# Opening tile's fourth head pair turned earlier, first products on PSUM tiles of their own, second tile's keys turned on two PSUM tiles and its queries last

## The chip, the cores and the metric

The kernel runs on one core of a Trainium2 chip. The metric is device time in microseconds (us), lower is better; before the change three runs gave 329.65, 330.06 and 330.78 us, median 330.06. A core has a matrix engine (PE, with its weight loads shown as PEld), a vector engine (DVE), an activation engine (ACT), a general engine (POOL) and a queue engine (SP). Each runs its own instructions strictly in the order in which they are written; engines wait for one another on semaphores. POOL also issues most of the input transfers, so whatever waits on POOL holds up the transfers queued behind it.

## The reference

Sliding-window causal attention (8 batches, 8 heads, 576 positions, head size 64, window 64), followed by a gated feed-forward block on 4608 tokens of 512 channels:

```python
scores = scale * np.matmul(q, k.transpose(0, 1, 3, 2))
mask = (rel >= 0) & (rel < window)
scores = np.where(mask, scores, -1000000000.0)
attn = np.exp(scores - max); attn = attn / (sum + 1e-09)
x = matmul(attn, v)   # heads side by side: 4608 x 512
g = x @ w_gate
out = ((g * sigmoid(g)) * (x @ w_val)) @ w_out   # d_ff = 1536
```

(Shortened; `max` and `sum` run over the keys.)

## The kernel before

**Tiles.** The 4608 tokens are nine tiles of 512: tile t is the first 512 positions of batch t, and tile 7 (LAST) gathers the last 64 positions of all batches. For each tile the kernel makes scores, exponentials and totals, multiplies by V (the mix), divides by the totals (`scale`, DVE, L385, which writes xT), runs twelve gate/value steps (`gate_value`, eight matmuls of 128x128 by 128x512 each; L429) and then the output projection (`project`, L438), which for tile t is woven into the attention of tile t+1. `gate_end` turns a step's two PSUM results into a slice of hT: a SiLU on ACT (L422), then a product on DVE (L423). The eight heads are handled as four pairs, u = 0 to 3.

**PSUM.** There are eight banks. Banks 0 and 1 belong to one tile, `two[0]`, banks 2 and 3 to `two[1]`; banks 4 to 7 are tiles of their own (`one0` to `one3` in the instruction order, all shown as `one` in the profile). Waits are made per tile: a write to bank 1 waits for a reader of bank 0. `out_tile()` and `d_tile()` alternate between banks 4/5 and 6/7 by counters in `taken`; a gate/value step takes one of each.

**Opening.** Tile 0 is read in fp32 and cast (`cast_first`, L544). Its q and k are turned by PE transposes (`turn_first`, L195), whose results are copied to queries and keys by DVE (L553 and, as `split_k`, L198). A bias for the mask is put into PSUM by matmuls (`bias_first`, L227), the scores are added (`scores_first`, L240), ACT takes the exponential (`weigh_first`, L558), totals come from matmuls with ones (`sums_first`, L295), and ACT inverts them by a logarithm (L316) and an exponential (L319). The products with V (`part_first`, L348) come in three passes, even, odd and late, with a tiny matmul and a tiny DVE copy (`marker`, `seen`) between the first two, which serve as a fence. Pair 3 is turned last (L195 at 12.5 us), its products go to bank 5 and are woven into the first gate matmuls (`gate_part`, L409), which run as soon as each pair is scaled.

**Second tile.** Tile 1's keys come in bf16 as `raw_k` (shown as k_r) and are turned on PE between gate steps 6 and 7 (pairs 0 and 1, banks 0 and 1) and between steps 8 and 9 (pairs 2 and 3, banks 2 and 3), L677, each followed by a DVE copy (L198). Its queries are turned by DVE itself (`turn_q`, L207), after half of each block has been moved between partitions (`second_halves`, L118: once on ACT, twice on POOL, once on DVE). From tile 2 on, DVE turns both (`turn`: L207 and L217), four pairs per tile, after chosen gate steps (`turns`).

**Transfers.** POOL's queue issues, in order, V of tile 0, the gate and value weights in blocks of 256 columns, tile 1's keys and queries among them, the output weights, V of tile 1, then q and k of tile 2. An issue waits for the landing of the transfer eight places earlier.

Of the kernel before, what the change touches and what calls it, by code (L numbers as in the profile page):

```python
# [10 lines left out]
BF16 = mybir.dt.bfloat16  # L11
# [6 lines left out]
def kernel(  # L18
# [10 lines left out]
    nc = tc.nc  # L29
# [24 lines left out]
    v1 = v12[:, 0]  # L54
# [21 lines left out]
    def load_runs(eng, dst, src, t, hs):  # L76
        eng.dma_start(
            dst.rearrange("r h e d -> r h (e d)"),
            src[batch(t), hs, 0:512].rearrange("h (r e) d -> r h (e d)", e=4),
        )  # L80
# [24 lines left out]
    def load_plain(t, us):  # L105

        for a in range(2):
            nc.gpsimd.dma_start(
                staged[t][0][64 * a:64 * a + 32, us],
                q[batch(t), a + 2 * us.start:2 * us.stop:2, 0:512]  # L110
                .rearrange("u (r e) d -> r u (e d)", e=16),
            )

    def second_halves(t, us, a, copy):

        src, dst = slice(64 * a, 64 * a + 32), slice(64 * a + 32, 64 * a + 64)
        ap = staged[t][0][:, us].rearrange("r u (e d) -> r (u e) d", d=D)
        copy(ap[dst, :, 0:32], ap[src, :, 32:64])  # L118
# [60 lines left out]
    def weights_gv(f0, f1, c0=0, c1=4):  # L179
        for src, dst in ((moe_w_gate, wg), (moe_w_val, wv)):  # L180
            nc.gpsimd.dma_start(
                dst[:, c0:c1, f0:f1],
                src[P * c0:P * c1, f0:f1].rearrange("(c r) f -> r c f", r=P),
            )

    def weights_o(c0, c1):
        nc.gpsimd.dma_start(
            wo[:, c0:c1, :],
            moe_w_out[P * c0:P * c1].rearrange("(c r) f -> r c f", r=P),
        )  # L190
# [3 lines left out]
        for e in range(4):  # L194
            nc.tensor.transpose(tp[:, P * e:P * e + P], src[:, e], identb[:])  # L195

    def split_k(dst, tp):
        nc.vector.tensor_copy(  # L198
            dst.rearrange("p (r e) -> p r e", e=4),
            tp.rearrange("p (e r) -> p r e", e=4),  # L200
        )
# [20 lines left out]
    def bias_first(u):  # L222

        for c in range(2):
            for h in range(2):
                r = slice(64 * h, 64 * h + 64)
                nc.tensor.matmul(  # L227
                    two[u % 2][64 * c:64 * c + 64, h], identb[r, r],
                    bias[r, c ^ h].rearrange("r e i c x -> r (e i c x)"),
                    start=True, stop=False,  # L230
                )
# [109 lines left out]
    def part_first(us, banks, x, ms):  # L341

        for u, b in zip(us, banks):
            E = weights[0, u]
            for m in ms:
                r = slice(0, P) if m % 2 else half(x)
                for h in range(2):
                    nc.tensor.matmul(  # L348
                        blocks(bank[b][half(h)], 0, m, m + 1),
                        v1[r, m // 2 if m % 2 or not x else m // 2 - 1, 2 * u + h, :],  # L350
                        blocks(E[r, h, :], 0, m, m + 1),
                        start=m + x == 0, stop=(m, x) == (6, 1),
                    )
# [153 lines left out]
    def keep_warm(n):  # L507
        for _ in range(n):
            nc.tensor.matmul(warm[0:D], ones[:, 0:D], ones[:])
# [33 lines left out]
    def cast_first(copy, u, i):  # L543
        copy(  # L544
            first[:, i, u].rearrange("r e (h d) -> r h e d", h=2),
            raw[i][:, 2 * u:2 * u + 2],
        )

    def turn_first(u, banks):
        tps = [bank[b].bitcast(BF16)[:, 0:512] for b in banks]  # L550
        for i in range(2):
            transposes(tps[i], first[:, i, u])
        (on_v if u else on_a)(queries[0][:, u, :], tps[0])  # L553
        split_k(kT[0][:, u, :], tps[1])
# [6 lines left out]
    def sums_first(u, b):  # L561
        totals_first(u, bank[b])
        inverse[0, u] = room(1)[:, 0]
        return lambda: log(inverse[0, u], bank[b]), lambda: invert(inverse[0, u])
# [12 lines left out]
    cast_first(on_a, 2, 0)  # L577
    cast_first(on_p, 3, 0)
    weights_gv(0, 256, 0, 2)
    on_p(v1[:, 0], v_first[:, 0])  # L580
    on_p(v1[:, 1], v_first[:, 1])
    weights_gv(0, 256, 2, 4)
    weights_gv(256, 512)
    weights_gv(512, 768)
# [5 lines left out]
    load_runs(nc.gpsimd, raw_k[:, 0:4], k, 1, slice(0, 4))  # L590
    weights_gv(1024, 1280)
    load_runs(nc.gpsimd, raw_k[:, 4:8], k, 1, slice(4, 8))
    load_plain(1, lo)
    weights_gv(1280, 1536)
    weights_o(0, 2)
    second_halves(1, lo, 1, on_p)
    load_plain(1, hi)
    weights_o(2, 4)
    weights_o(4, 8)
    weights_o(8, 12)  # L600
    load_halves(nc.gpsimd, vb[1], 1, range(3))
# [1 line left out]
    load_halves(nc.gpsimd, vb[1], 1, range(3, H))  # L603

    cast_first(on_v, 2, 1)
    bias_first(1)
    log0, inv0 = sums_first(0, 6)
    scores_first(1)
# [2 lines left out]
    inv0()  # L611
    keep_warm(1)
    turn_first(2, (4, 5))
    cast_first(on_v, 3, 1)
    bias_first(2)
    keep_warm(1)
    log1, inv1 = sums_first(1, 7)
    scores_first(2)
    log1()
    weigh_first(2)  # L620
    turn_first(3, (4, 5))
    bias_first(3)
    scores_first(3)
    weigh_first(3)
    inv1()
    even, odd, late = (0, 2, 4, 6), (1, 3, 5, 7), (2, 4, 6)
    log2, inv2 = sums_first(2, 6)
    part_first(range(3), (0, 1, 4), 0, even)
    marker(7)
    nc.vector.tensor_copy(seen[:], bank[7][0:D, 0:1])  # L630
    part_first(range(3), (0, 1, 4), 0, odd)
    marker(7)
    part_first(range(3), (0, 1, 4), 1, late)
    log2()
    inv2()
    part_first((3,), (5,), 0, even)
    log3, inv3 = sums_first(3, 7)
    log3()
    inv3()
    part_first((3,), (5,), 0, odd)  # L640
    pairs = [(bank[2], bank[3]), (bank[6], bank[0])]
    scale(0, 0, bank[0])
    scale(0, 1, bank[1])
    gate_part(0, (0, 1), pairs, 0)
    marker(7)
    part_first((3,), (5,), 1, late)
    gate_part(0, (0, 1), pairs, 1)
    for u in (2, 3):
        scale(0, u, bank[u + 2])
    for c in range(2, 4):  # L650
        gate_part(0, (0, 1), pairs, c)
    taken["v"] = 1
    set_silu()
    for m in range(12):
        if m < 2:
            gate_end(0, m, pairs[m])
        else:
            gate_value(0, m)
        if m == 2:
            for x in range(2):  # L660
                for c in range(2):
                    nc.vector.tensor_copy(
                        mask[half(x), 0, c],
                        tri[half(x), x ^ c].rearrange("r (y e) -> r e y", e=16),
                    )
            for i in (1, 2, 4):
                nc.vector.tensor_copy(mask[:, i:2 * i], mask[:, 0:i])
            for E in eb:
                nc.vector.memset(E[:, 0], 0.0)
        if m == 8:  # L670
            second_halves(1, lo, 0, on_a)
        if m in (6, 8):
            for u in (m - 6, m - 5):
                tp = bank[u].bitcast(BF16)[:, 0:512]
                for e in range(4):
                    for h in range(2):
                        nc.tensor.transpose(  # L677
                            tp[half(h), P * e:P * e + P], raw_k[:, 2 * u + h, e], identb[:]
                        )
                split_k(kT[1][:, u, :], tp)  # L680
        if m in (9, 10):
            turn_q(1, m - 9)

    set_exp()
    second_halves(1, hi, 0, on_v)
# [4 lines left out]
    def columns(c0, c1):  # L690
        project_part(0, range(4), tiles, range(c0, c1))

    scores(1, 0)
    columns(0, 4)
    scores(1, 1)
    columns(4, 7)
    for w in range(2):
# [9 lines left out]
    for t in range(1, NT):  # L707
        if t > 1:
            set_exp()
            scores(t, 0)  # L710
            project(t - 1, 0)
            if t == 2:
                stage_v(3)
            o_ps = out_tile()
            project_part(t - 1, (1,), (o_ps,), range(5))
            scores(t, 1)
            sums(t, 0)
            project_part(t - 1, (1,), (o_ps,), range(5, 12))
            project_end(t - 1, 1, o_ps)
            project(t - 1, 2)  # L720
            sums(t, 1)
            mix_all(t)
            project(t - 1, 3)
        set_silu()
        if t + 1 == LAST:
            load_last_v()
        elif t + 1 < NT and t > 1:
            cast_v(t + 1)
        if t + 2 < NT:
            load_qk(t + 2)  # L730
            if t > 1 and t + 2 != LAST:
                stage_v(t + 2)
        if t == 2:
            k_l = load_k(
                cast.tile([P, 4, 4, 4 * D], BF16, name="k_l", tag="c0"),
                [(b, S - P) for b in range(4, 8)],
            )
        turns = (6, 8, 10, 11) if t == 1 else (1, 4, 7, 10)
        for m in range(12):
            gate_value(t, m)  # L740
            if m in turns and t + 1 < NT:
                turn(t + 1, turns.index(m))
            if m == 8 and 3 <= t < 7:
                turn_k(kT[2], k_l, t - 3)
# [32 lines left out]
```

## Time and profile before

| What | us |
|---|---|
| Median of three runs | 330.06 |
| The profiled execution, its own time | 330.95 |
| Its span, first to last instruction | 329.2 |
| PE busy | 318.4 (97%) |
| DVE busy | 217.8 (66%) |
| ACT busy | 165.8 (50%) |
| POOL busy | 148.4 (45%) |
| Granted PE clock, mean | 1.000 |

The profiled execution is 0.89 us longer than the median of the runs, and 1.75 us of it lie outside the span. Rows of the timeline read: start, duration, engine, line, operation, out<-in, shape, count, and in brackets the idle time before it and what ended it. Consecutive matmuls overlap: one 128x512 matmul takes 0.38 us, but the next starts 0.216 us after it, so 16 of them fill 3.46 us, and a gate/value step of eight fills 1.73 us. The chain of work that ended last is read from the end backwards to what released each piece.

### The profile page before, as it was taken

To read this page: it belongs to the slowest core of one execution; us is meant where nothing else is said; L and a number is where in the kernel's file an instruction comes from. 1 tells how busy PE (TensorE), PEld (TensorE's weight loads), DVE (VectorE), ACT (ScalarE), POOL (GpSimd) and SP (SyncE) were. 2 spreads that over 40 slices of the span, in tenths; PEclk is the share of its full clock that TensorE was granted. 3 is DMA by queue.
4 is the path that set the end of the run, shared out by engine and by line. 5 is a ranking of instruction groups with operands and counts; after the bars stand their busy time and mean duration, and the time that the engine had idled before them with its cause. 6 is when DMAs were issued, how large, how long until landed. Compare 5 with 4: busy or idle time off the path is not lost.

```text
span 329.2 us, 7015 instructions
## 1 busy us (share of the span) xinstructions
PE 318.4 (97%) x2739; PEld 151.8 (46%) x2782; DVE 217.8 (66%) x344; ACT 165.8 (50%) x237; POOL 148.4 (45%) x263
## 2 busy tenths in 40 slices
PE   7998899999999999999999999999999999999995
PEld 4544444444444454445444444445444544444443
DVE  3565575479767776687669767876787666774422
ACT  4762367435833574356535663475337633683310
POOL 4872956887055697556422989474110000000000
PEclk9999999999999999999999999999999999999999
DMA  7999999999589999969950999899601300021013
GB/s 244 178 176 198 165 164 183 197 150 131 116 157 197 163 152 181 205 69 183 219 86 7 140 195 99 57 175 191 127 3 26 91 16 0 9 81 44 0 24 105
DMA packets 83522, 40.36 MB, mean 123 GB/s; under 512 B 64160, under 2 KB 78752, under 8 KB 83488
## 3 DMA queue, kind: packets, MB, share of 16 engines
q0 software_dynamic: 51488, 22.59, 57.8%
q1 hardware_dynamic: 31456, 16.79, 21.0%
q10 hardware_dynamic: 544, 0.52, 0.5%
q8 instruction: 21, 0.34, 0.4%
q14 instruction: 13, 0.11, 0.1%
HBM read 53.02 MB, written 9.44 MB: 190 GB/s over the span
## 4 chain that ended last, share of the span: by engine, by line
PE 93%; DVE 4%; issue 1%; DMA 1%; ACT 0%; DVEq 0%
PE one L429 55%; PE one L438 27%; PE two L269 2%; PE two L369 2%; PE one L302 1%; DMA q_f<-in_q_dram 1%; DVE hT L423 1%; PE one L195 1%; PE two L409 1%; PE one L480 1%; DVE kT L198 1%; PE two L240 0%; DVE kT L217 0%; DVE qT L207 0%; PE two L227 0%
## 5 line engine op out<-in xcount | busy, mean ns | idle before, releaser
L422 ACT ACTIVATE sg<-one 128x512 f32<-128x512 f32 x107 | 63.9, 597 | 116.8 <-PE one L429 90.8
L423 DVE TENSOR_TENSOR hT<-sg,one 128x512 bf16<-128x512 f32 x106 | 73.6, 694 | 62.3 <-PE one L429 61.4
L429 PE MATMUL one<-xT,wg 128*128 128x512 bf16 x415 | 108.4, 379 | 0.9
L429 PE MATMUL one<-xT,wv 128*128 128x512 bf16 x415 | 107.2, 379 | 0.1
L438 PE MATMUL one<-wo,hT 128*128 128x512 bf16 x396 | 93.5, 380 | 1.5 <-issue 0.3
L126 POOL DMA_DIRECT2D k_s<-in_k_dram x112 | 60.7, 549 | 24.2 <-DMA q_s<-in_q_dram 16.6
L429 PEld LDWEIGHTS <-wv 128*128 128x128 bf16 x424 | 41.5, 98 | 50.0
L429 PEld LDWEIGHTS <-wg 128*128 128x128 bf16 x424 | 41.3, 98 | 49.9 <-issue 0.3
L438 PEld LDWEIGHTS <-hT 128*128 128x128 bf16 x420 | 39.1, 98 | 46.5 <-issue 1.8
L282 ACT ACTIVATE eb<-two 128x960 bf16<-128x960 f32 (+1 forms) x32 | 29.5, 974 | 15.9 <-PE two L269 15.8
L217 DVE STREAM_TRANSPOSE kT<-k_s 128x512 bf16<-128x512 bf16 x28 | 36.1, 1288 | 0.0
L285 DVE TENSOR_TENSOR eb<-eb,mask 128x960 bf16<-128x960 bf16 (+1 forms) x32 | 21.1, 659 | 11.7 <-ACT eb L282 11.6
L177 POOL CAST vb<-v_f 128x512 bf16<-128x512 f32 x20 | 11.5, 619 | 36.9 <-DMA v_f<-in_v_dram 14.7
L385 DVE TENSOR_TENSOR xT<-two,r 128x512 bf16<-128x512 f32 x34 | 21.7, 686 | 6.4 <-PE two L369 4.8
L319 ACT ACTIVATE r<-r 128x512 f32<-128x512 f32 (+1 forms) x34 | 22.3, 655 | 1.0
L207 DVE STREAM_TRANSPOSE qT<-q_s 128x512 bf16<-128x512 bf16 x32 | 22.4, 703 | 0.1
L316 ACT ACTIVATE r<-one 128x512 f32<-128x512 f32 x32 | 18.9, 590 | 6.1 <-PE one L302 5.3
L91 POOL DMA_DIRECT2D q_s<-in_q_dram x24 | 13.0, 556 | 4.7 <-DVE qT L207 4.7
L290 DVE TENSOR_TENSOR both<-eb 128x512 bf16<-128x512 bf16 x32 | 13.6, 425 | 1.1
L152 POOL DMA_DIRECT2D vb<-in_v_dram x16 | 11.1, 715 | 4.6 <-DMA vb<-in_v_dram 2.0
L488 ACT ACT_TABLE_LOAD x9 | 11.5, 1283 | 2.0 <-issue 1.9
L98 POOL DMA_DIRECT2D q_s<-in_q_dram x16 | 8.6, 627 | 7.0 <-DVE qT L207 7.0
(117 smaller groups left out, 197.4 us busy)
## 6 DMA issues: line engine op xcount, KB each, us to landing
k_s<-in_k_dram POOLq DMA_DIRECT2D x112, 56.0 KB, 4.8
q_s<-in_q_dram POOLq DMA_DIRECT2D x24, 248.0 KB, 5.3
v_f<-in_v_dram SPq DMA_DIRECT2D x40, 128.0 KB
wg<-in_moe_w_gate_dram POOLq DMA_DIRECT2D x5, 256.0 KB, 8.1
wv<-in_moe_w_val_dram POOLq DMA_DIRECT2D x5, 256.0 KB, 8.7
q_f<-in_q_dram SPq DMA_DIRECT2D x4, 256.0 KB
wo<-in_moe_w_out_dram POOLq DMA_DIRECT2D x2, 512.0 KB, 9.0
vb<-in_v_dram POOLq DMA_DIRECT2D x16, 64.0 KB, 5.4
```

Source lines behind the costliest of these rows:

```text
L126: nc.gpsimd.dma_start(k_s[p0:p0 + 32, g, :, 0:w], k[b, a:H:2, s:s + P].rearrange("u (r e) d -> r u (e d)", e=4) [:, :, 32 * c:32 * c + w],)
L207: nc.vector.transpose(queries[t][:, u, :].rearrange("r (e x) -> r e x", e=16), staged[t][0][:, u].rearrange("r (e d) -> r e d", d=D)[:, :, ...
L217: nc.vector.transpose(dst[:, u, :].rearrange("r (g x e) -> r g e x", g=4, e=4), k_s[:, :, u].rearrange("r g (e d) -> r g e d", d=D)[:, :, ...
L282: nc.scalar.activation(flat, s_ps[h][:].rearrange("r a b -> r (a b)")[:, 0:n], AF.Exp, scale=0.125)
L285: nc.vector.tensor_mul(flat, flat, mask[:].rearrange("r j c e y -> r (j c e y)")[:, 0:n])
L316: nc.scalar.activation(r, d_ps, AF.Ln)
L319: nc.scalar.activation(r, r, AF.Exp, scale=-1.0)
L385: nc.vector.tensor_mul(x, o_ps, r)
L422: nc.scalar.activation(sg[:], g_ps[:], AF.Silu)
L423: nc.vector.tensor_mul(hT[t][:, m, :], sg[:], v_ps[:])
L429: nc.tensor.matmul(ps[:], w[:, c, P * m:P * m + P], xT[t][:, c, :], start=(c == 0), stop=(c == 3),)
L438: nc.tensor.matmul(o_ps[:], hT[t][:, c, P * s:P * s + P], wo[:, c, :], start=(c == 0), stop=(c == 11),)
```

## The change

- Pair 3's key cast moves up on DVE, and its transposes move ahead of pair 1's totals and pair 2's scores, on banks 6 and 7. Pair 1's totals go to bank 2 (in `two[1]`). Two filler matmuls (`keep_warm`) become one.
- The two casts of tile 0's V leave POOL for DVE, after the last key copy.
- The products of pairs 0 to 3 go to banks 4, 5, 0 and 1, with pair 3's even products ahead of the fence. The first gate matmuls are no longer woven with products: after all products come 16 in a row, on banks 2 and 3 (`two[1]`) and 4 and 6.
- Tile 1's keys: pairs 0 and 1 are still turned after step 6, pairs 2 and 3 now after step 9; the two pairs of a step stand in `two[0]` and `two[1]`. The copies after step 9 are on ACT instead of DVE.
- Tile 1's queries: loads and half moves are issued later on POOL's queue (behind the last gate weights and the first output weights); the half move of pairs 0 and 1 that was POOL's is DVE's, after step 9; ACT's half move and both turns stand after step 10 instead of at steps 8, 9 and 10.
- The first column of the projection of tile 0 (four matmuls) stands ahead of tile 1's first scores.
- Tile 2's turns during tile 1 stand after steps 6, 7, 9 and 10 instead of 6, 8, 10 and 11.

```diff
--- before.py
+++ after.py
@@ -194,8 +194,8 @@
         for e in range(4):
             nc.tensor.transpose(tp[:, P * e:P * e + P], src[:, e], identb[:])
 
-    def split_k(dst, tp):
-        nc.vector.tensor_copy(
+    def split_k(dst, tp, copy=nc.vector.tensor_copy):
+        copy(
             dst.rearrange("p (r e) -> p r e", e=4),
             tp.rearrange("p (e r) -> p r e", e=4),
         )
@@ -577,8 +577,6 @@
     cast_first(on_a, 2, 0)
     cast_first(on_p, 3, 0)
     weights_gv(0, 256, 0, 2)
-    on_p(v1[:, 0], v_first[:, 0])
-    on_p(v1[:, 1], v_first[:, 1])
     weights_gv(0, 256, 2, 4)
     weights_gv(256, 512)
     weights_gv(512, 768)
@@ -590,12 +588,11 @@
     load_runs(nc.gpsimd, raw_k[:, 0:4], k, 1, slice(0, 4))
     weights_gv(1024, 1280)
     load_runs(nc.gpsimd, raw_k[:, 4:8], k, 1, slice(4, 8))
+    weights_gv(1280, 1536)
     load_plain(1, lo)
-    weights_gv(1280, 1536)
     weights_o(0, 2)
-    second_halves(1, lo, 1, on_p)
+    weights_o(2, 4)
     load_plain(1, hi)
-    weights_o(2, 4)
     weights_o(4, 8)
     weights_o(8, 12)
     load_halves(nc.gpsimd, vb[1], 1, range(3))
@@ -603,6 +600,7 @@
     load_halves(nc.gpsimd, vb[1], 1, range(3, H))
 
     cast_first(on_v, 2, 1)
+    cast_first(on_v, 3, 1)
     bias_first(1)
     log0, inv0 = sums_first(0, 6)
     scores_first(1)
@@ -611,45 +609,39 @@
     inv0()
     keep_warm(1)
     turn_first(2, (4, 5))
-    cast_first(on_v, 3, 1)
     bias_first(2)
-    keep_warm(1)
-    log1, inv1 = sums_first(1, 7)
+    turn_first(3, (6, 7))
+    log1, inv1 = sums_first(1, 2)
     scores_first(2)
     log1()
     weigh_first(2)
-    turn_first(3, (4, 5))
     bias_first(3)
     scores_first(3)
     weigh_first(3)
     inv1()
+    for i in range(2):
+        on_v(v1[:, i], v_first[:, i])
+    log2, inv2 = sums_first(2, 6)
     even, odd, late = (0, 2, 4, 6), (1, 3, 5, 7), (2, 4, 6)
-    log2, inv2 = sums_first(2, 6)
-    part_first(range(3), (0, 1, 4), 0, even)
+    aos = (4, 5, 0, 1)
+    part_first(range(4), aos, 0, even)
     marker(7)
     nc.vector.tensor_copy(seen[:], bank[7][0:D, 0:1])
-    part_first(range(3), (0, 1, 4), 0, odd)
+    part_first(range(3), aos, 0, odd)
     marker(7)
-    part_first(range(3), (0, 1, 4), 1, late)
+    part_first(range(2), aos, 1, late)
     log2()
     inv2()
-    part_first((3,), (5,), 0, even)
     log3, inv3 = sums_first(3, 7)
     log3()
     inv3()
-    part_first((3,), (5,), 0, odd)
-    pairs = [(bank[2], bank[3]), (bank[6], bank[0])]
-    scale(0, 0, bank[0])
-    scale(0, 1, bank[1])
-    gate_part(0, (0, 1), pairs, 0)
-    marker(7)
-    part_first((3,), (5,), 1, late)
-    gate_part(0, (0, 1), pairs, 1)
-    for u in (2, 3):
-        scale(0, u, bank[u + 2])
-    for c in range(2, 4):
+    part_first((3,), aos[3:], 0, odd)
+    part_first((2, 3), aos[2:], 1, late)
+    pairs = [(bank[2], bank[3]), (bank[4], bank[6])]
+    for c in range(4):
+        scale(0, c, bank[aos[c]])
         gate_part(0, (0, 1), pairs, c)
-    taken["v"] = 1
+    taken["g"] = taken["v"] = 1
     set_silu()
     for m in range(12):
         if m < 2:
@@ -667,19 +659,22 @@
                 nc.vector.tensor_copy(mask[:, i:2 * i], mask[:, 0:i])
             for E in eb:
                 nc.vector.memset(E[:, 0], 0.0)
-        if m == 8:
-            second_halves(1, lo, 0, on_a)
-        if m in (6, 8):
-            for u in (m - 6, m - 5):
-                tp = bank[u].bitcast(BF16)[:, 0:512]
+        if m in (6, 9):
+            for i in range(2):
+                u = m // 9 * 2 + i
+                tp = two[i].bitcast(BF16)[:, 0, 0:512]
                 for e in range(4):
                     for h in range(2):
                         nc.tensor.transpose(
                             tp[half(h), P * e:P * e + P], raw_k[:, 2 * u + h, e], identb[:]
                         )
-                split_k(kT[1][:, u, :], tp)
-        if m in (9, 10):
-            turn_q(1, m - 9)
+                split_k(kT[1][:, u, :], tp, on_v if m == 6 else on_a)
+        if m == 9:
+            second_halves(1, lo, 1, on_v)
+        if m == 10:
+            second_halves(1, lo, 0, on_a)
+            for u in range(2):
+                turn_q(1, u)
 
     set_exp()
     second_halves(1, hi, 0, on_v)
@@ -690,8 +685,9 @@
     def columns(c0, c1):
         project_part(0, range(4), tiles, range(c0, c1))
 
+    columns(0, 1)
     scores(1, 0)
-    columns(0, 4)
+    columns(1, 4)
     scores(1, 1)
     columns(4, 7)
     for w in range(2):
@@ -735,7 +731,7 @@
                 cast.tile([P, 4, 4, 4 * D], BF16, name="k_l", tag="c0"),
                 [(b, S - P) for b in range(4, 8)],
             )
-        turns = (6, 8, 10, 11) if t == 1 else (1, 4, 7, 10)
+        turns = (6, 7, 9, 10) if t == 1 else (1, 4, 7, 10)
         for m in range(12):
             gate_value(t, m)
             if m in turns and t + 1 < NT:
```

## The prediction

> **What bounds the kernel now.** I read the page first: PE is busy 97% of the span, so after the opening nothing shortens the run but matmuls taken away (none are, save one filler) or PE waits. I then followed the chain from the start and looked for pieces that are not PE's:
>
> ```profile
> 29.93 0.69 DVE hT L423
> 30.61 0.61 DVE kT L198
> 31.27 0.41 PE two L677 x8
> ...
> 35.35 0.69 DVE hT L423
> 36.04 0.61 DVE kT L198
> 36.69 0.41 PE two L677 x8
> ...
> 80.85 0.43 DVE both L290
> 81.27 0.58 DVE eb L285
> 81.88 0.44 DVE both L290
> 82.35 0.40 PE one L302 x2
> ```
>
> Between 21 and 77 us the first two DVE pieces are the largest breaks: PE turned one pair's keys, then stood until DVE had read them, since the second pair's bank belongs to the same tile. The third is tile 2's totals, which wait for a DVE that was still turning tile 2. What each break costs is read from the stretches between gate steps:
>
> ```profile
> 21.00:29.66 8.66, 8.61 (x40) 3.79 (x39) 5.37 (x17) 3.86 (x7) 4.05 (x6) 1.00 1.45 195
> 29.66:31.61 1.95, 0.84 (x17) 0.56 (x16) 1.29 (x2) 0.00 (x0) 0.00 (x0) 1.00 1.29 203
> 35.08:37.04 1.96, 0.85 (x18) 0.56 (x17) 1.29 (x2) 1.00 (x1) 1.96 (x4) 1.00 1.09 177
> ```
>
> (Stretch, length, then busy time and count of PE, PEld, DVE, ACT, POOL, granted clock, DMA share, GB/s.) Steps 2 to 6 fill 8.66 us without a hole; each visit to the keys takes 1.95 us of PE for 0.84 us of work.
>
> The opening, by the timeline:
>
> ```profile
> 7.70 1.04 PE L195 MATMUL one<-identb,qk_b 128*128 128x128 bf16 x8
> 10.59 0.62 PE L195 MATMUL one<-identb,qk_b 128*128 128x128 bf16 x8
> 13.37 0.69 DVE L198 COPY kT<-one 128x512 bf16<-128x512 bf16 x1
> 14.12 0.41 PE L240 MATMUL two<-qT,kT 64*64 64x128 bf16 x16 [0.44 <-DVE kT L198]
> 14.59 1.02 ACT L558 ACTIVATE eb<-two 128x1024 bf16<-128x1024 f32 x1 [0.91 <-PE two L240]
> 17.13 0.38 PE L409 MATMUL two<-xT,wg 128*128 128x512 bf16 x1 [0.27 <-DVE xT L385]
> 21.02 0.38 PE L429 MATMUL one<-xT,wg 128*128 128x512 bf16 x1
> ```
>
> Pair 3's keys reach SBUF at 14.06, its exponential ends at 15.61, and step 2 begins at 21.02, 3.89 us after the first gate matmul, though 16 matmuls need 3.46. The reader should also see that the same eight transposes take 1.04 us early and 0.62 later, while the granted clock reads 1.00 in every stretch.
>
> **The change part by part.**
>
> *Opening: -0.84.* DVE casts pair 3's keys at 9.8 (0.42, L544), so PE turns pair 3 behind pair 2's bias: 8 transposes of 0.056 from 11.4 to 11.8. Pair 1's totals follow; pair 2's scores wait for its key copy (ends 12.13, unchanged) and start at 12.2, as before. The logarithm of pair 1 now reads `two[1]` and runs 12.3 to 12.9 (0.60), and pair 3's bias waits behind it: that is a new wait, and PE's scores of pair 3 queue behind it. DVE copies pair 3 at 12.05 (0.42, then 0.69): keys ready at 13.06. Bias at 13.0, scores at 13.2, ready 13.6. ACT runs pair 2's exponential 12.85 to 13.85, then pair 3's, 13.75 to 14.8, instead of 15.61. DVE's two V casts (0.42 each) end by 13.9. PE: totals of pair 2 at 13.9, even products of pairs 0 to 2 (24 in 0.40), those of pair 3 from 14.85, marker, odd products (0.40), second marker behind `seen` at 15.45, late products of pairs 0 and 1, pair 3's totals and remaining products, to 16.4. `scale` of pair 0 waits only for bank 4: 15.95 to 16.65, so the gate starts at 16.7; the other scales follow every 0.61 us, the last held by pair 3's inverse (logarithm and exponential end at 17.6) until 18.5, ahead of its matmuls at 19.3. 16 in a row: step 2 at 20.18, against 21.02. Bounds: -1.1, if the fence hides wholly; -0.3, if the casts take the 0.84 that one took beside a POOL cast (12.04) and push the even products past 14.8. The filler that goes lay in a gap, worth 0.
>
> *The POOL queue.* Without its casts POOL issues weights about 1.8 us sooner. By the trace's landing events step 2's value weights came at 20.85, and they would now be used at 21.04; so zero, even if nothing comes sooner. The port is a place where row and rule differ: POOL's weight issue at 9.34 took 0.70 us beside a DVE cast (9.38 to 9.79), and the next, at 10.03 with no cast, 0.71. The Trainium skill's page SBUF — State Buffer, section SBUF: two separate sides, says that a DVE copy from fp32 in its fast mode locks POOL out of writing descriptors for queue-issued transfers; by it two casts would hold the weights up by some 0.84 us, and the sum below would read 0.6 us higher. I go by the row.
>
> *Keys in two tiles: -2.54.* PE goes from the first pair straight to the second. The 1.95 us contain 0.09 before the first group and 0.34 from the second group's start (31.27) to step 7 (31.61); a first group without a wait adds at most 0.25 (8 half-width transposes, pairwise beside each other, 0.056 each). That leaves 0.68, saving 1.27 at each visit. Bounds: 1.15 and 1.4. The earlier readers of both tiles are long done; the keys landed at 27.7 and 31.7, and are needed at 28.8 and 34.5. After step 9 ACT copies: no row shows ACT with this stride; between ACT's plain copy, 0.59 (L553), and its half move, 1.04 (L118), I take 0.59, the same shape. Then SiLU 10 isn't late.
>
> *Queries last, first column early: +0.65.* Call E the end of step 11 on PE, about 38.8. ACT's half move (1.04) comes after SiLU 10 and ends at E-0.7; DVE's two turns (0.70, pitch 0.63) then run to E+0.65, and hT of step 11 behind them, E+0.6 to E+1.27. PE now has four projection matmuls first. They use all four banks, and the fourth one's bank is the one that this hT reads: PE waits at E+0.65 until E+1.3, and tile 1's scores queue behind. Before, the scores (42.32) stood ahead and hid hT. Bounds: 0.35 (hT on time) and 1.25 (ACT copies of 1.04, or queries landing late). Next is no loss: the second scores come 3.2 us after the first; pairs 2 and 3 are turned by E+3.2, needed at E+4.8, and the exponentials, 1.83 us for two, begin when the table load (1.28, behind SiLU 11) is long done. POOL's remaining half move waits for the last queries with five V loads behind it; V of tile 1 landed at 49.94 for a use at 53.3, and POOL no longer stops 4.4 us for its first half move, so this stays covered. DVE's added half move (0.42) fits in the 1.0 us it has free per step.
>
> *Tile 2's turns: -0.57.* From tile 2's first scores (77.02) to its first gate matmul (90.68) are 13.66 us; in tile 3, from 111.49 to 124.58, 13.09. A turn of a pair sets hT back 0.60 (70.90 instead of 70.30). With turns after 6 and 7, hT 8 is 1.2 late; PE needs its bank for step 10's value at 74.34, hT 8 would end at 73.9: no stall. After turns at 9 and 10 hT 11 is 1.28 late, and DVE is free when the exponential arrives, instead of a further turn later. All of 0.57 goes; bounds 0 and 0.57. Tile 2's keys must have landed (66.74 before) when DVE wants them, 69.8 less the gains: 66.9; they move forward with POOL's queue.
>
> *Sum:* -0.84 - 2.54 + 0.65 - 0.57 = -3.30. On the profiled execution 330.95 becomes 327.65; the median of the runs lies 0.89 lower: 326.8. All best ends give -4.1 (326.0), all worst -1.35 (328.7).
>
> **The rivals.**
>
> 1. *The late queries cost their upper end*, 1.25, and tile 2 gains nothing: -2.13, 327.9. For it: three engines in a row stand before that fourth matmul. Against: each is short in its row.
> 2. *ACT binds the opening.* The new wait behind pair 1's logarithm takes back most of it: -0.3, 327.3. For it: ACT is busy 8.74 of 11 us from 10 to 21. Against: pair 3's exponential has 0.8 us to gain.
> 3. *More:* hT is on time and the opening reaches its best end: 326.1.
> 4. *The key waits stay*, because another reader of `two` holds PE: without the 2.54, 329.3. Against: the last readers are gate step 0's product and DVE copies from three steps before.
> 5. *Slower: the PE clock.* One filler goes and PE waits 0.4 us at two or three new places by 15 us. If PE fell back to the early pace (0.106 per transpose against 0.056, half rate), each us of work would cost another; it decides from 3.3 us of work upward, and 6 us would give 326.8 + 6 = 332.8. Against: the pauses before, 0.44 and 0.27, changed nothing in the pitch.
> 6. *Transfers late:* tile 2's keys don't move forward and DVE waits with hT behind it: about +1.2, 328.0.
>
> **How the numbers follow.** Forecast 0.45 (own range 326.3 to 327.3); rivals 1 to 6: 0.15, 0.13, 0.11, 0.03, 0.07, 0.06. A measurement here tells about 0.3% (1 us) from no change. Faster: all but 4 and 5, less a little for what I don't see, 0.88; same 0.05 (rival 4 and some of 1); slower 0.07. The range leaves out rivals 4 and 5 and reaches from the best end, less half a us for the runs' own spread, to the worst end: 325.5 to 328.7.
>
> **What would show it.** Right: step 2 near 20.2; no DVE piece in the chain beside L677, with step 7 some 0.7 us after step 6's slot; a PE wait of about 0.6 at L438 for hT before tile 1's first scores; tile 2's totals without a wait. Wrong: 128-wide transposes at 0.106 after 11 us; a PE wait for a transfer in steps 2 to 5; an ACT copy of keys near 1 us; PE waiting in steps 8 to 11 of tile 1.

## The result and the profile after

The changed kernel takes 326.6 us (median of 4 runs, 326.01 to 327.05) where the kernel before took 329.97 (4 runs, 329.65 to 330.78): ratio 0.9893, interval 0.9868 to 0.9918, so 3.4 us less. A second set of the same kernel gave 326.4 against 330.11, ratio 0.9883 (0.9864 to 0.9903). The forecast was 326.8. The profiled execution has its own time of 326.34 and a span of 324.4, against 330.95 and 329.2.

The chain of waits after, up to the stretch in which the one before had its third DVE break:

```profile
39.13 0.55 PE two L269 x30
...
77.29 0.55 PE two L269 x32
77.84 0.22 PE one L302 x4
```

Followed back, this chain reaches to 38.70 us, and between there and 90 us no DVE piece is left in it; tile 2's totals (L302) follow its scores without a wait. It doesn't reach the two visits to the keys, which lie earlier; these are read from the stretches. The same stretches as before, by windows (the key transposes are L668 now):

```profile
18.88:27.54 8.66, 8.61 (x40) 3.82 (x39) 5.68 (x17) 3.86 (x7) 4.22 (x7) 1.00 1.45 196
27.54:28.20 0.66, 0.66 (x17) 0.48 (x17) 0.39 (x1) 0.00 (x0) 0.49 (x1) 1.00 1.44 194
33.39:34.05 0.66, 0.66 (x17) 0.48 (x17) 0.39 (x1) 0.11 (x1) 0.66 (x2) 1.00 1.24 205
```

Steps 2 to 6 still fill 8.66 us, and each visit to the keys takes 0.66 us, all of it work, instead of 1.95 with 0.84 of work. The wait that was to take its place is there too, in the timeline ahead of tile 1's scores:

```profile
37.52 0.81 PE L438 MATMUL one<-wo,hT 128*128 128x512 bf16 x3
38.05 0.65 DVE L423 TENSOR_TENSOR hT<-sg,one 128x512 bf16<-128x512 f32 x1
38.76 0.38 PE L438 MATMUL one<-wo,hT 128*128 128x512 bf16 x1 [0.43 <-DVE hT L423]
39.06 0.62 PE L269 MATMUL two<-qT,kT 64*64 64x128 bf16 x32
```

The fourth matmul of the first column starts at 38.76 where its slot was 38.17, a loss of 0.59 us. The opening is different from what the two spans suggest:

```profile
4.77 0.62 PE L195 MATMUL one<-identb,qk_b 128*128 128x128 bf16 x8 [0.26 <-ACT qk_b L544]
8.81 0.62 PE L195 MATMUL one<-identb,qk_b 128*128 128x128 bf16 x8
9.42 0.66 DVE L544 CAST qk_b<-k_f 128x512 bf16<-128x512 f32 x1 [0.72 <-DMA k_f<-in_k_dram]
10.91 0.60 ACT L316 ACTIVATE r<-two 128x512 f32<-128x512 f32 x1 [0.72 <-PE two L295]
11.53 1.95 ACT L558 ACTIVATE eb<-two 128x1024 bf16<-128x1024 f32 x2
18.90 1.03 PE L429 MATMUL one<-xT,wg 128*128 128x512 bf16 x4
```

Step 2 (the first L429) begins 2.12 us sooner than the 21.02 before. But pair 2's transposes, the third L195 group and the last PE work that stands in the same place in both kernels, already begin 1.78 us sooner, at 8.81 instead of 10.59: PE ran at its quicker pace from the first group on (0.62 us for eight transposes), where the profile of before shows 1.04, 1.04 and 0.62. The first group began 0.40 us sooner (4.77, before 5.17), the pace gives the other 1.38. Nothing that was changed lies ahead of that point on PE. The unchanged kernel, profiled again, has that start at 9.16. So every kernel below is read from that start, called T3. In us, from the rows of each timeline (an idle stretch of PE counts in the column where it lies):

| Kernel | T3 | T3 to step 2 | step 2 to scores (1,1) | T3 to end of span |
|---|---|---|---|---|
| before | 10.59 | 10.43 | 25.41 | 318.6 |
| before, again | 9.16 | 10.35 | 25.41 | 318.5 |
| after | 8.81 | 10.09 | 23.41 | 315.6 |
| after, again | 8.88 | 9.88 | 24.06 | 316.0 |

Here scores (1,1) is the second group of tile 1's scores. Two more lines of the comparison: from tile 2's first scores to its first gate matmul are 13.08 us (72.90 to 85.98), before 13.66.

Summed from T3, the profiled pair gives -0.34 (opening) - 2.59 (two visits: 1.95 + 1.96 - 2 x 0.66) + 0.59 (first column) - 0.58 (tile 2) = -2.92; the rows themselves give 318.6 - 315.6 = 3.0.

### The profile page after: what moved, and what is told of

It is laid out like the page before. It is cut to its first block, busy times and chain, and to the rows that moved or that the text cites. A ratio compares the mean times of both kernels' runs of the same rounds, so it can differ in the third digit from the quotient of the medians.

```text
span 324.4 us, 7013 instructions
## 1 busy us (share of the span) xinstructions
PE 315.9 (97%) x2737; PEld 150.9 (47%) x2780; DVE 217.8 (67%) x345; ACT 167.0 (51%) x239; POOL 146.3 (45%) x260
## 4 chain that ended last, share of the span: by engine, by line
PE 86%; issue 1%; DVE 0%
PE one L429 51%; PE one L438 28%; PE two L269 3%; PE two L369 2%; PE one L302 1%; PE one L480 1%; PE two L302 0%; DVE os__4138 L484 0%
## 5 line engine op out<-in xcount | busy, mean ns | idle before, releaser
L429 PE MATMUL one<-xT,wg 128*128 128x512 bf16 x414 | 108.1, 379 | 0.9
L429 PE MATMUL one<-xT,wv 128*128 128x512 bf16 x416 | 107.3, 379 | 0.1
L429 PEld LDWEIGHTS <-wv 128*128 128x128 bf16 x424 | 41.5, 98 | 50.0
L429 PEld LDWEIGHTS <-wg 128*128 128x128 bf16 x424 | 41.3, 98 | 49.9 <-issue 0.3
```

The lines of the kernel that those rows point to most:

```text
L429: nc.tensor.matmul(ps[:], w[:, c, P * m:P * m + P], xT[t][:, c, :], start=(c == 0), stop=(c == 3),)
```

## The experiments

**The unchanged kernel, a second look.** Is the early T3 the change's doing, or one execution's?

> The kernel before, unchanged, for a second profile. Theory (the two profiled executions differ by 1.2 us ahead of any changed instruction, because PE reached full pace at 9 to 10 us in the one and before 5 us in the other, which varies from run to run): PE's third group of transposes starts anywhere from 8.8 to 10.6, and step 2 comes 10.4 us after it, whatever the pace before. Rival (the kernel before is always slow early, the change makes PE fast earlier): third group at 10.6 again, early transposes at 1.04 us a group.

One run: 329.44 us, span 327.7, T3 at 9.16, step 2 10.35 later. So the early pace of PE differs between executions of one kernel, and 1.4 of the 4.8 us between the two spans are found there. Whether it is slow as often in both kernels, one execution can't tell (see the end of the next part).

**The opening alone.** The old kernel with the new opening:

```diff
-    on_p(v1[:, 0], v_first[:, 0])
-    on_p(v1[:, 1], v_first[:, 1])
...
+    cast_first(on_v, 3, 1)
...
+    turn_first(3, (6, 7))
+    log1, inv1 = sums_first(1, 2)
...
+    aos = (4, 5, 0, 1)
+    part_first(range(4), aos, 0, even)
```

> The kernel before with the changed opening alone (pair 3 turned sooner, V cast on DVE, products on banks 4, 5, 0, 1, sixteen gate matmuls in a row); keys, queries, first column, turns and the loads of tile 1 as before. Theory (the term of -0.84 us in the sum): 329.97 - 0.84 = 329.1 us, and step 2 starts 0.8 us earlier than in a run of before whose PE is at full pace from the same moment. Rival (the two profiled executions taken at their word, step 2 at 18.90 against 21.02): -2.1 us, 327.9.

329.54 us (11 runs; before 329.92, 17 runs), ratio 0.9984 (0.9973 to 0.9996): 0.4 us, half of what was expected, though the interval (0.1 to 0.9 us) doesn't exclude the 0.84; the rival's 2.1 is excluded. Its T3 to step 2 is 9.98, which is 0.4 better than before; but its second visit to the keys is longer. Timeline of this kernel:

```profile
33.49 0.69 DVE L423 TENSOR_TENSOR hT<-sg,one 128x512 bf16<-128x512 f32 x1 [1.46 <-PE two L670]
34.83 0.41 PE L670 MATMUL two<-identb,k_r 128*64 128x128 bf16 x8 [1.53 <-DVE kT L198]
```

PE waits 1.53 us here; the first visit of the same kernel shows 1.10. DVE takes up this hT 0.43 us later than what the profile shows it waiting for, and the key copy, with PE behind it, is late by that. T3 to end is therefore 318.6, as before, so the 0.4 us of the medians can't be seen in this one profile as a whole.

**Everything but the opening.** The new kernel with the old opening, the V casts back on POOL:

> The opening of before with the rest of the change (keys of a step in two PSUM tiles, ACT copies after step 9, queries last, first column ahead of the scores, loads moved, turns after 6, 7, 9, 10). Theory: -2.54 + 0.65 - 0.57 = -2.46 us, 327.5; the pauses at the keys are 0.68 instead of 1.95 us, and tile 2's totals do not wait. Rival (the opening carries 2.1 of the 3.4 us): -1.3 us, 328.7.

326.93 us (4 runs), ratio 0.9907 (0.9893 to 0.9921): 3.0 us by the medians, 2.4 from T3 to end (316.2). Expected was 2.46; the rival's 1.3 is excluded. Step 2 to scores (1,1) takes 23.64, which is 23.41 and some weight waiting (0.19 at step 2). So the second tile is where nearly all of the gain lies.

**The keys on one PSUM tile.** The new order, but both pairs of a visit on two banks of the same tile:

```diff
-                tp = two[i].bitcast(BF16)[:, 0, 0:512]
+                tp = two[m // 9].bitcast(BF16)[:, i, 0:512]
```

> The changed kernel with the two pairs of a key step in the two banks of one PSUM tile again (two[0] after step 6, two[1] after step 9). Theory (the wait is the reader of the other bank of the same tile): each visit to the keys takes 1.9 us of PE again instead of 0.66, +2.5, 329.0. Rival (the wait went because DVE no longer copies behind hT or because the keys land earlier): 326.5 to 327.

328.18 us (6 runs), ratio 0.9941 (0.9925 to 0.9957), 1.6 to 1.8 above the two medians of after. The rival, that the order alone was enough, falls. Waits of this kernel, by its timeline:

```profile
29.06 0.41 PE L668 MATMUL two<-identb,k_r 128*64 128x128 bf16 x8 [1.11 <-DVE kT L198]
35.15 0.59 ACT L198 COPY kT<-two 128x512 bf16<-128x512 bf16 x1 [0.61 <-PE two L668]
35.79 0.41 PE L668 MATMUL two<-identb,k_r 128*64 128x128 bf16 x8 [0.68 <-ACT kT L198]
```

And the two visits of the same kernel by windows, from the end of the last step's slot to the next step:

```profile
27.45:29.41 1.96, 0.85 (x18) 0.56 (x17) 1.29 (x2) 0.00 (x0) 0.95 (x2) 1.00 1.45 196
34.60:36.13 1.53, 0.85 (x17) 0.56 (x17) 1.12 (x2) 0.59 (x1) 1.17 (x2) 1.00 1.17 206
```

The first visit costs 1.96 us again. The second costs 1.53, less than expected: ACT's copy doesn't stand behind an hT as DVE's does, so it starts right behind the transposes. Together +2.17 against 2 x 0.66. From step 2 to the end its trace takes 307.7 us where after's takes 305.5, the same 2.2; the medians show less, and in this trace the opening is 0.35 us shorter than in after's.

**Tile 2's turns as before.** `turns` for t = 1 back to the old list:

```diff
-        turns = (6, 7, 9, 10) if t == 1 else (1, 4, 7, 10)
+        turns = (6, 8, 10, 11) if t == 1 else (1, 4, 7, 10)
```

> The changed kernel with tile 2 turned after steps 6, 8, 10 and 11 again. Theory (the term of -0.57): +0.57, 327.2, with tile 2's totals waiting for DVE again. Rival (tile 2's wait went because its keys landed earlier, or because the queries of tile 1 moved): 326.6, no wait at the totals.

327.24 us (6 runs), ratio 0.9924 (0.9907 to 0.994), 0.6 to 0.8 above after. From tile 2's first scores to its first gate matmul: 13.65 (72.57 to 86.22), against 13.08, and the totals wait for DVE again:

```profile
77.90 0.40 PE L302 MATMUL one<-both,ones 64*64 64x512 bf16 x2 [0.17 <-DVE both L290]
```

The 0.57 is shown.

**Pair 3 turned late.** The rest of the new opening stays:

```diff
-    turn_first(3, (6, 7))
     log1, inv1 = sums_first(1, 2)
     scores_first(2)
     log1()
     weigh_first(2)
+    turn_first(3, (6, 7))
     bias_first(3)
```

> The changed kernel with pair 3's transposes back behind pair 2's exponential (as before the change), all else as changed. Theory (turning sooner is what gains in the opening): pair 3's exponential 0.7 us later, step 2 10.5 us or more after the third group of transposes, 326.6 + 0.6 = 327.2. Rival (the gain comes from sixteen gate matmuls in a row): 326.8, within 0.2 of the changed kernel.

327.16 us (6 runs), ratio 0.9917 (0.99 to 0.9934), 0.6 to 0.8 above after. In its trace T3 to step 2 is 11.49, which is 1.4 worse than after and even 1.1 worse than the old order; step 2 to end is the same 305.5. Read from the order: the even products of all four pairs now stand ahead of the one fence, so a late pair 3 holds every pair: in this trace the last even products wait for its exponential until 14.50, and the fence stands behind them.

**The V casts left on POOL.** Does moving them matter, when the prediction costed it at nothing?

```diff
     weights_gv(0, 256, 0, 2)
+    on_p(v1[:, 0], v_first[:, 0])
+    on_p(v1[:, 1], v_first[:, 1])
...
-    for i in range(2):
-        on_v(v1[:, i], v_first[:, i])
```

> The changed kernel with tile 0's two V casts back on POOL, between the first weight loads. Theory of the prediction (the POOL queue costed at zero): no change, 326.5 us, step 2's value weights landing just ahead of their use. Rival (with the shorter opening step 2 comes at 18.9 while these weights land at 20.1 to 20.9 behind the casts, as in the kernel before, so the freed queue is what lets the opening gain): PE waits 0.5 to 1 us for the weights in step 2, 327.2.

327.57 us (6 runs), ratio 0.9916 (0.99 to 0.9932), 1.0 to 1.2 above after: the wait that the rival named is there. Its timeline around step 2:

```profile
10.62 0.63 POOL L580 CAST v<-v_f 128x512 bf16<-128x512 f32 x1
11.75 0.61 POOL L581 CAST v<-v_f 128x512 bf16<-128x512 f32 x1 [0.50 <-DMA v_f<-in_v_dram]
12.31 0.70 POOL L181 DMA_DIRECT2D wg<-in_moe_w_gate_dram  x1
19.11 1.04 PE L429 MATMUL one<-xT,wg 128*128 128x512 bf16 x4
20.55 1.04 PE L429 MATMUL one<-xT,wv 128*128 128x512 bf16 x4 [0.41 <-DMA wv<-in_moe_w_val_dram]
```

The cast waits 0.50 us for V, and the weights are issued behind it. Step 2 starts 0.14 us behind its slot (18.97) and its value half 0.58 behind (20.55 instead of 19.97): 0.72 in all. The trace thus shows 0.7 of the 1.0; the rest was not found (the profiled execution, 326.95, was the fastest of its six). That the new kernel is close to this edge is seen in its own second profile:

```profile
20.27 1.04 PE L429 MATMUL one<-xT,wv 128*128 128x512 bf16 x4 [0.48 <-DMA wv<-in_moe_w_val_dram]
```

**The same kernel, three more runs and another profile**, for the size of such differences.

> The changed kernel, unchanged, timed beside its variants on one chip and profiled again. Theory: 326.6 us, step 2 9.7 to 10.1 us after PE's third group of transposes, first scores of tile 1 20.2 us after step 2, and the PE wait ahead of them 0.4 to 0.6. Rival: early pace slower in this execution, then the whole opening shifts by up to 1.3 us and nothing else.

326.4 us; its trace has the weight wait just shown (0.65 on the step), which the first profile hasn't. By these two profiles alone, this kernel and the one with the casts on POOL can't be told apart: T3 to the end of the span is 316.0 in both. That the casts on POOL cost 1.0 us rests on the medians, and the interval there (0.9900 to 0.9932) overlaps a little with those of after (up to 0.9918 and 0.9903).

**Scores ahead of the first column.** The order of before at this place, with the late queries:

```diff
-    columns(0, 1)
     scores(1, 0)
-    columns(1, 4)
+    columns(0, 4)
```

> The changed kernel with tile 1's first scores ahead of the first projection column, as before the change. Theory (the scores then wait for DVE's turns, which end 0.6 us after step 11, as long as the column waited for hT): 326.5, no change, a PE wait of 0.6 moved from the column to the scores. Rival (the column ahead of the scores was the gain): 327.2.

326.14 us (4 runs), ratio 0.9875 (0.9859 to 0.9892), no worse than after. PE row of its timeline:

```profile
38.19 0.62 PE L269 MATMUL two<-qT,kT 64*64 64x128 bf16 x31 [0.33 <-DVE qT L207]
```

The scores now wait for the queries (the first at 37.62, the rest at 38.19), as long as the fourth matmul waited for hT. Step 2 to scores (1,1) is 23.38 against 23.41. The early column alone buys nothing: it exchanges one wait for another.

**Two half columns ahead of the scores.** In both orders PE asks for something that DVE isn't done with: the bank from which DVE still reads the value result of step 11 for hT, or the queries. Two columns on the two banks that step 10 left free (token groups s = 0 and 1) need neither:

```diff
-    columns(0, 1)
+    project_part(0, (0, 1), tiles[:2], range(0, 2))
     scores(1, 0)
-    columns(1, 4)
+    project_part(0, (2, 3), tiles[2:], range(0, 2))
+    columns(2, 4)
```

> The changed kernel, but the four projection matmuls ahead of tile 1's first scores are two columns on the two banks that steps 10 left free (s = 0 and 1) instead of one column on all four banks; the other two banks follow after the scores. Same work. Theory (the +0.65 term: PE waits at the fourth matmul for hT of step 11, measured 0.59 in the profile): that wait goes, 326.6 - 0.6 = 326.0, first scores 0.6 us earlier, and all later work with them. Rival (DVE's turns or POOL's half move hold the scores anyway, or the wait comes back at the second scores): 326.6, no change.

325.56 us (4 runs, 325.52 to 326.15), ratio 0.9871 (0.9859 to 0.9884). Once more:

> The variant with two columns on two banks once more, beside the others, to confirm the best kernel: theory 325.7 us, 0.6 below the changed kernel; rival: 326.4, its first result was a matter of the runs.

325.60 us (4 runs), ratio 0.9866 (0.9845 to 0.9887). Chain of waits of this second run:

```profile
35.89 1.73 PE one L429 x8
37.62 0.86 PE one L438 x4
38.48 0.55 PE two L269 x27
39.03 2.70 PE one L438 x12
```

Four matmuls, then the scores, with no wait: 0.59 us sooner than in after, counted from step 2. This is the fastest of the kernels here by its median, 0.8 to 1.0 below after.

**One column more ahead of the totals.** On top of the last edit, `columns(4, 7)` became `columns(4, 8)` and `columns(7, 10)` became `columns(8, 10)`:

> The variant with two columns on two banks ahead of tile 1's first scores, and in addition one projection column (four matmuls, 0.86 us) moved from behind tile 1's totals to ahead of them. Theory: the totals' wait for DVE (0.5 us at L302 in all kernels so far) is covered: 325.6 - 0.5 = 325.1. Rival (ACT's logarithms and inverses behind the totals start 0.35 us later and hold scale and the first gate step): 325.6, no change.

325.76 us (4 runs), ratio 0.9874 (0.9856 to 0.9893): nothing. Its timeline:

```profile
45.83 0.63 PE L302 MATMUL two<-both,ones 64*64 64x512 bf16 x8
49.36 0.61 PE L369 MATMUL two<-eb,vb 64*64 64x128 bf16 x32 [0.54 <-ACT r L316]
```

The totals no longer wait (0.63 us for what took 1.02 in the kernel without this edit), but ACT starts on them later, and the products wait 0.54 us for its logarithm.

## Why the prediction was right or wrong

**The total was right**, -3.3 against -3.4 and -3.7, and three of the terms were right to a tenth. That the total is so close is in part luck: the opening gave about half of its term, and a gain that the working doesn't speak of, ahead of T3 (see the last paragraph), makes up for it.

- *Keys in two tiles*, -2.54: 0.66 us per visit against 0.68 predicted, so -2.59. One tile brings back 1.96 and 1.53. Rival 4, that another reader keeps the wait, falls.
- *Queries last, first column early*, +0.65: 0.59, at the named matmul and for the named hT. ACT's key copy took 0.59, as taken. Rival 1 falls. But the reasoning was incomplete: the step was costed as the price of the early column, and with the column behind the scores it costs the same (326.14). Late queries cost it in either order, and it can be had back: step 2 to scores (1,1) takes 25.41 us before, which is 22.82 without the 2.59 of the two visits; after takes 23.41, and with two half columns it is 22.82 again.
- *Tile 2's turns*, -0.57: 0.58, and 0.57 in the other direction.

**The opening was mis-sized**, -0.84 predicted. The traces give 0.34 in after and 0.4 alone. The step that failed is "DVE casts pair 3's keys at 9.8 (0.42, L544)" with pair 2's key copy ending "unchanged". In the new order that cast stands on DVE ahead of pair 2's copies, and its data weren't there: DVE waits 0.72 us for the transfer, and starts at 9.42. The prediction took it as ready because in the profile of before PE was so slow that T3 lay at 10.59, well behind the landing (in the traces with the new opening the cast starts at 9.2 to 9.5). The cast also took longer than the 0.42 worked with, 0.66 in after (the row at 9.42 above), but not in the second profile of the same kernel:

```profile
9.49 0.43 DVE L544 CAST qk_b<-k_f 128x512 bf16<-128x512 f32 x1 [0.98 <-DMA k_f<-in_k_dram]
```

The traces with the new opening and the early turn line up by this (from T3, in us; start and length of the cast, end of pair 2's key copy, start of pair 2's exponential on ACT, step 2):

| Kernel | cast | its length | pair 2's keys | exponential | step 2 |
|---|---|---|---|---|---|
| predicted | -0.8 | 0.42 | 1.54 | 2.26 | 9.59 |
| one column more | 0.13 | 0.43 | 1.53 | 2.39 | 9.74 |
| two half columns | 0.17 | 0.43 | 1.53 | 2.39 | 9.74 |
| the same, again | 0.24 | 0.68 | 1.85 | 2.39 | 9.74 |
| turns as before | 0.36 | 0.43 | 1.72 | 2.39 | 9.74 |
| one PSUM tile | 0.39 | 0.43 | 1.75 | 2.39 | 9.74 |
| after, again | 0.61 | 0.43 | 1.97 | 2.49 | 9.88 |
| opening alone | 0.71 | 0.43 | 2.06 | 2.59 | 9.98 |
| scores ahead | 0.59 | 0.68 | 2.19 | 2.71 | 10.08 |
| after | 0.61 | 0.66 | 2.20 | 2.72 | 10.09 |

(The kernel with the casts on POOL has 1.53 and 9.88, of which 0.14 is its wait for weights.) Up to 1.85 step 2 doesn't move; from there it moves by as much as pair 2's keys do. In after 0.12 us of this come from the late start of the cast (as in after, again) and 0.23 from its length. So the opening is worth 0.67 us (10.41, the mean of the three traces with the old opening, less 9.74) when the keys are there, and 0.3 in after, where they come late. This last is read from the spread of the traces; no kernel was run in which the keys land sooner. Where pair 2's keys don't hold it, ACT does, as in two half columns:

```profile
11.06 0.60 ACT L316 ACTIVATE r<-two 128x512 f32<-128x512 f32 x1 [0.43 <-PE two L295]
11.56 1.93 ACT L558 ACTIVATE eb<-two 128x1024 bf16<-128x1024 f32 x2
```

Pair 1's logarithm waits for pair 1's totals and starts 1.89 after T3, where 1.71 was worked out; both exponentials stand right behind it, and pair 3's ends 4.32 after T3 where 4.21 was worked out. That is the other 0.15 (9.74 against 9.59), and it is rival 2 in small. As a whole rival 2 was named for -0.3, and the opening came close to it in after, but mostly by another mechanism, the late cast.

**The POOL queue at zero was wrong in its cover.** The working said that the weights, at 20.85, come in time for a use at 21.04 "even if nothing comes sooner". With step 2 at 18.9 that cover is gone: left on POOL, the casts cost 1.0 us by the medians, 0.7 of it seen in the trace. The sum came out since the casts did move. A cover must be looked at where the work will lie after the change, not where it lay. As to the rule of the Trainium skill, SBUF — State Buffer, section SBUF: two separate sides, that a DVE copy of that kind locks POOL out of writing descriptors: the issue beside DVE's V casts, at 11.94 in after, took 0.79 us and the issue at 13.42, beside no DVE work, 0.80; the 0.6 us that the prediction estimated from it did not appear. A smaller effect is in other rows: the issue beside the V casts took 0.81 in after, again (at 11.45) and 0.90 in one column more (at 11.97), where the next ones took 0.76 and 0.75; and pair 3's key cast took 0.66 in after, where the issue beside it took 0.70 (at 9.16), but 0.43 in after, again, where that issue took 0.79 (at 9.27).

**Rivals 3, 5 and 6 fall.** For rival 3 hT would have had to be on time, and it cost 0.59 (its own terms also add up to 326.2, not 326.1). Eight transposes take 0.62 us from T3 on in every trace where they don't wait in between (0.83 in after's pair 3, whose key half waits for the cast). Tile 2's keys have landed at 61.89 instead of 66.74, V of tile 1 at 46.08 instead of 49.94.

**What stays open.** From T3 on the profiles show 2.5 to 3.0 us of gain, the medians 3.4 to 3.7. The spans alone shrank by as much as the medians: 39 runs of the kernel before have 327.5 to 329.3 us, median 328.1, and eight of after 324.2 to 324.9, median 324.4. If the stretch from T3 on takes what the profiles show, 0.7 to 1.2 us of this lie ahead of T3 in the typical run, where nothing was changed on PE. So it isn't excluded that the slow start of PE is more frequent in the kernel before; no run shows why that would be. The 0.43 us by which DVE is late at one hT in the kernel with the opening alone has no cause in its profile. The working named step 2 "near 20.2" as the sign of a right opening; it came at 18.90 for another reason, the pace of PE, and read alone it would have confirmed too much.

## What to carry to other kernels

Compare two profiles from the last instruction that the change can't have moved, not from the start of the span: here 1.8 of 4.8 us lay ahead of it. When a stage is pulled forward, list the transfers that its lateness had hidden, and check each against the new time; a cast moved ahead on an in-order engine makes everything behind it wait for the cast's own data. Where PE waits for one reader of a PSUM tile with two banks, give each result a tile of its own; and where a wait remains, look for work whose inputs and banks are already free, as the two half columns were.

## What the runs showed of the hardware

PE ran its first microseconds at half pace, eight transposes in 1.04 us instead of 0.62, for a time that differed between executions: the first group in both profiles of the unchanged kernel (1.04 and 0.97) and the second too in its first, none in after. The granted clock in the windows reads 1.00 in both. T3 varied from 8.76 to 10.59 us, mostly by this. The Trainium skill, TensorE: Matmul & The Clock Gate, section The HAM clock gate (the "warmup" mystery), describes such a start at half rate and a change-over that depends on where in a free-running window the first matmul lands, with a spread of half a microsecond. The direction agrees, while the spread here is larger: full pace is there by 4.77 us in after, and in the first profile of before the four bias matmuls at 8.66 still take 0.64 us where they take 0.41 at 11.14.

The weight transfers arrived about 1.3 us apart in after (by the landing events of its trace 16.34, 17.64 and 18.97) while the windows show 196 GB/s. A single landing can still differ by as much between executions: in after's second profile the issue of step 2's value weights came 0.31 us later (13.00 instead of 12.69) and the landing 1.25 later (20.22 instead of 18.97), 2.82 behind the transfer ahead of it and only 0.64 ahead of the next.
